# Seven products of halves in place of eight, in three groups of one feed-forward stage

## The chip, the cores and the metric

The kernel runs on one core of one Trainium2 chip. The metric is device time in microseconds of one execution, the median of several runs. A core has TensorE (PE: matmuls; PEld: its weight loads), VectorE (DVE), ScalarE (ACT), GpSimd (POOL) and SyncE (SP), which here issues most DMAs. Each engine works through its own queue in order.

## The reference

Two parts, all in float32 (the feed-forward weights arrive as float64):

```python
# attention: batch 8, heads 12, seq 448, head_dim 64
q_n, k_n = rmsnorm(q, g_q), rmsnorm(k, g_k)
attn = softmax(q_n @ k_n.T / 8)                   # per batch and head
attn_out = attn @ v
x = attn_out.transpose(0, 2, 1, 3).reshape(3584, 768)
# feed-forward: d_model 768, d_ff 1536
g, val = x @ w_gate, x @ w_val
out = (g / (1 + exp(-g)) * val) @ w_out           # (3584, 768)
```

## The kernel before

**Blocks.** The eight batches are taken two at a time, in four blocks `n` = 0 to 3 (the text calls them blocks 1 to 4). A block has an *up* stage (gate and value, `x @ w_gate` and `x @ w_val`), then a *down* stage (`@ w_out`) between whose products the attention of the next block is laid. The last block has no attention beside it.

**Fifteen products.** Both stages use a bilinear scheme for block matrices: a block of 2 batches x 3 thirds of the model width, times a 3 x 3 arrangement of the weights, is formed of 15 products of sums in place of 18. The 15 sums on the side of `x` lie in `xs[:, SLOT[x], c, :]` (128 partitions, `c` = two halves of the contraction of 256, 448 tokens); the sums of the weights are made once, at the beginning, and kept in DRAM (`up_sides`, `down_sides`). `UP_SUMS` and `BLOCKS` give their order there.

**An up stage.** It runs over four groups `g` (128 of the output columns of a third each). In a group, each of the 15 steps of `UP_ORDER` has two products, for the gate and for the value (`which`), and each product is two matmuls (`c` = 0, 1) of a 128 x 128 weight against 448 columns; a float32 matmul is two instructions in the trace. The gate's go to the PSUM banks `mm`, the value's to `at`; within each pair of banks the steps alternate (`b`). After each step its bank is read (L1409 to L1415): by ScalarE where `UP_READ` says `COPY` (6 steps), else by VectorE, which adds it to or takes it from a partial result in SBUF (9 steps), with one further sum per 15 steps (L1528, `add_d`). A bank's next product waits for that read (`free[bank]`). When a gate's result is complete ScalarE forms its SiLU (L1551), and VectorE multiplies it with the value (L1554, `weigh`, into `gt`).

**Weights on the way.** Five steps' weights come in one load into one of two `ws` buffers (L1428), on SP. A load waits in SP's queue for the products that used the buffer before.

**Hand-over.** The down stage's operands are sums of the results (`combine`, L1185 and L1189). `combine(6)` and `combine(1)` are made for each group as soon as its results are there, into `hs`; the first two down products use them.

**The order of the work** is made by `Order`, a planner in the kernel. Each piece of work has an engine, an assumed time, a due time (`when`), what it comes after, and which buffers it takes or uses. The planner lays the pieces out by those assumed times and emits them engine by engine in the order that results. Its times are not seen by the chip: there, only the order in each queue and the waits on data are left. `block_start`, `block_end` and `UP` give the due times; a `rank` moves a piece ahead. `port=True` marks GpSimd work and VectorE work with operands in SBUF, which the planner keeps apart.

## Time and profile before

| | us |
|---|---|
| median of 3 runs | 1454.96 |
| lowest, highest | 1453.89, 1457.8 |
| profiled execution: span from the first to the last instruction | 1452.0 |
| up stage of block 4 in it | 1173.8 to 1354.4 |
| down stage of block 4 and the tail | 1354.4 to 1452.0 |

The page gives no other time of the profiled execution than its span. In the tables that follow, a row of a *group* of instructions has line, engine, operation, tiles (out <- in), shape and count, then the group's busy time, the mean of one in ns, and the idle time of its engine just before them with what ended it. A row of the *timeline* has start, length (both us), engine, line, operation, tiles, shape and count. A row of the *stage table* has the busy time and count of each engine in a stretch, TensorE's granted clock, the DMA share and GB/s. A row of *DMA issues* has size and the median time from issue to landing. A row of *waits* has the total in us, the times and the longest.

### The profile page before, as it was taken

To read this page: it belongs to the slowest core of one execution; us is meant where nothing else is said; L and a number is where in the kernel's file an instruction comes from. 1 tells how busy PE (TensorE), PEld (TensorE's weight loads), DVE (VectorE), ACT (ScalarE), POOL (GpSimd) and SP (SyncE) were. 2 spreads that over 40 slices of the span, in tenths; PEclk is the share of its full clock that TensorE was granted. 3 is DMA by queue.
4 is the path that set the end of the run, shared out by engine and by line. 5 is a ranking of instruction groups with operands and counts; after the bars stand their busy time and mean duration, and the time that the engine had idled before them with its cause. 6 is when DMAs were issued, how large, how long until landed. Compare 5 with 4: busy or idle time off the path is not lost.

```text
span 1452.0 us, 19362 instructions
## 1 busy us (share of the span) xinstructions
PE 1426.0 (98%) x6736; PEld 689.5 (47%) x6736; DVE 879.8 (61%) x1485; ACT 601.6 (41%) x1210; POOL 405.7 (28%) x476
## 2 busy tenths in 40 slices
PE   8999999999999999999999999999999999999997
PEld 4455454534444455544444455544444445555553
DVE  5889876878866434546877642455686644442533
ACT  6875444476653222356564122345555322212100
POOL 4756666625443000022443200011434300000000
PEclk9999999999999999999999999999999999999999
DMA  7778979854643533433644623443463452322235
GB/s 196 217 219 268 352 266 310 260 149 90 129 103 64 133 102 92 114 113 70 122 98 86 138 74 107 107 112 93 85 126 77 95 135 73 108 73 90 69 100 110
DMA packets 410416, 193.29 MB, mean 133 GB/s; under 512 B 280004, under 2 KB 390852, under 8 KB 410308
## 3 DMA queue, kind: packets, MB, share of 16 engines
q1 hardware_dynamic: 399040, 190.57, 49.1%
q10 hardware_dynamic: 11140, 1.38, 0.7%
q8 instruction: 55, 0.90, 0.3%
q14 instruction: 53, 0.43, 0.1%
q0 software_dynamic: 128, 0.00, 0.0%
HBM read 157.29 MB, written 34.60 MB: 132 GB/s over the span
## 4 chain that ended last, share of the span: by engine, by line
PE 90%; DMA 3%; DVE 2%; ACT 2%; SPq 1%; issue 1%; POOL 1%; ACTq 0%; DVEq 0%; POOLq 0%
PE at L1474 25%; PE mm L1474 25%; PE mm L1663 23%; PE at L1049 8%; PE st L970 7%; PE st L1080 1%; PE mm L1080 1%; DMA out_dram<-spare 1%; SPq L768 1%; DMA work<-in_k_dram 1%; ACT es L985 1%; DMA xs<-in_moe_w_gate_dram 0%; PE st L908 0%; DMA v<-in_v_dram 0%; ACT work L918 0%
## 5 line engine op out<-in xcount | busy, mean ns | idle before, releaser
L1474 PE MATMUL at<-xs,ws 128*128 128x448 f32 x960 | 401.2, 540 | 2.5 <-DVE v L1413 1.4
L1474 PE MATMUL mm<-xs,ws 128*128 128x448 f32 x960 | 401.7, 541 | 0.2 <-DVE hs L1315 0.2
L1474 PEld LDWEIGHTS at<-xs,ws 128*128 128x128 f32 x960 | 181.4, 190 | 184.7 <-issue 166.7
L1474 PEld LDWEIGHTS mm<-xs,ws 128*128 128x128 f32 x960 | 182.2, 190 | 180.7 <-issue 177.9
L888 POOL TENSOR_TENSOR work<-work,rr 128x448 f32<-128x448 f32 x72 | 71.8, 1016 | 467.5 <-DVE rr L715 341.6
L1663 PE MATMUL mm<-gt,ws 128*128 128x448 f32 x448 | 175.5, 543 | 0.0
L970 PE MATMUL st<-work 64*64 64x448 f32 (+1 forms) x1536 | 151.2, 501 | 10.3 <-ACT work L918 4.9
L985 ACT ACTIVATE es<-st 128x896 f32<-128x896 f32 x129 | 114.2, 914 | 101.6 <-PE at L1049 87.8
L1411 DVE TENSOR_TENSOR gt<-gt,mm 128x448 f32<-128x448 f32 x64 | 39.7, 621 | 188.1 <-PE mm L1474 161.7
L1663 PE MATMUL mm<-hs,ws 128*128 128x448 f32 x384 | 151.3, 544 | 0.0
L990 POOL TENSOR_TENSOR sums<-es 128x896 f32<-128x896 f32 x36 | 77.2, 2145 | 176.8 <-PE st L1080 83.7
L1663 PEld LDWEIGHTS mm<-gt,ws 128*128 128x128 f32 x448 | 83.6, 190 | 83.0 <-issue 80.8
L1551 ACT ACTIVATE st<-gt 128x448 f32<-128x448 f32 x96 | 52.3, 547 | 159.1 <-DVE gt L1415 85.7
L1409 ACT COPY gt<-mm 128x448 f32<-128x448 f32 x80 | 42.6, 532 | 157.5 <-PE mm L1474 157.4
L1049 PE MATMUL at<-es,v 64*64 64x448 f32 (+1 forms) x1032 | 106.0, 507 | 0.0
L1663 PEld LDWEIGHTS mm<-hs,ws 128*128 128x128 f32 x384 | 71.3, 190 | 71.0 <-issue 70.1
L970 PEld LDWEIGHTS st<-work 64*64 64x64 f32 x1536 | 50.9, 133 | 79.1 <-issue 37.4
L1409 ACT COPY v<-at 128x448 f32<-128x448 f32 x96 | 51.0, 532 | 80.4 <-PE at L1474 79.6
L990 POOL TENSOR_TENSOR sums<-sums,es 128x896 f32<-128x896 f32 x36 | 76.0, 2112 | 2.8
L1049 PEld LDWEIGHTS at<-es,v 64*64 64x64 f32 (+1 forms) x1032 | 44.1, 134 | 56.2 <-issue 50.4
L1554 DVE SCALAR_TENSOR_TENSOR gt<-st,v 128x448 f32<-128x448 f32 x96 | 59.7, 622 | 7.3 <-DVE v L1415 0.5
L1411 DVE TENSOR_TENSOR v<-v,at 128x448 f32<-128x448 f32 x64 | 39.8, 621 | 39.6 <-PE at L1474 39.5
(170 smaller groups left out, 1550.5 us busy)
## 6 DMA issues: line engine op xcount, KB each, us to landing
ws<-up_sides SPq DMA_DIRECT2D x32, 1024.0 KB, 5.6
ws<-down_sides SPq DMA_DIRECT2D x16, 1024.0 KB, 5.7
ws<-down_sides SPq DMA_DIRECT2D x28, 512.0 KB, 4.8
ws<-up_sides SPq DMA_DIRECT2D x16, 768.0 KB, 4.9
out_dram<-spare SPq DMA_DIRECT2D x168, 56.0 KB, 2.1
v<-in_v_dram SPq DMA_DIRECT2D x96, 96.0 KB, 2.5
ws<-up_sides SPq DMA_DIRECT2D x32, 256.0 KB, 5.9
ws<-up_sides SPq DMA_DIRECT2D x16, 512.0 KB, 5.8
```

Of the source, the lines that this page charges most:

```text
L888: nc.gpsimd.tensor_tensor(out=tiles["t", m][:, x], in0=tiles["qk", (m, x)], in1=rr.to_broadcast([P, NC, C]), op=ALU.mult,)
L970: nc.tensor.matmul(st[ds(D * x, D), h, 0:n], tiles["KT", m][rows, ds(P * j + D * of_keys, D)], tiles["QT", m][rows, ds(Q * of_queries, n)] ...
L985: nc.scalar.activation(e, tiles["st", (m, j)][:, :, 0 : S * width(j) // P], AF.Exp)
L990: nc.gpsimd.tensor_tensor(out=to, in0=tiles["e", (m, 0)] if j == 1 else to, in1=e, op=ALU.add)
L1049: nc.tensor.matmul(tiles["at", (m, x)][ds(D * h, D), ds(0, Q) if early else queries], tiles["v", m][rows, j, h], tiles["e", (m, j)][rows, ...
L1080: nc.tensor.matmul(to[ds(D * h + C * x, C)], halves[:, x] if half else many[:, 0:C], term[:, h, 0:Q] if half else term[:, h, ts(x, Q)], st ...
L1409: nc.scalar.copy(to, ps)
L1411: nc.vector.tensor_tensor(out=to, in0=old, in1=ps, op=ALU.add)
L1474: nc.tensor.matmul(ps(), w[:, which, c, at], xs[:, SLOT[x], c], start=fresh and c == 0, stop=c == NC2 - 1, skip_group_check=True,)
L1551: nc.scalar.activation(take(*act, [P, 2, TB])[:, 0, 0:S], to, AF.Silu)
L1554: nc.vector.scalar_tensor_tensor(to, tiles[act][:, 0, 0:S], 1.0 / SCALE, tiles[ready], op0=ALU.mult, op1=ALU.mult,)
L1663: nc.tensor.matmul(banks[s][:, 0:S], w[:, s, g, at], where[x][:, g], start=fresh and g == 0, stop=g == NG - 1, skip_group_check=True,)
```

## The change

**Halves.** In the last block (`SEVEN = {3: (1, 2, 3)}`), groups 1, 2 and 3 treat each of the 15 outer products as a 2 x 2 by 2 x 2 product: tokens in two halves of 224, the contraction in its two halves `c`, and gate and value as the two halves of the columns. That is eight products of 128 x 128 against 224 columns; the new code forms them of seven (Winograd's form), each with operands of its own: A11, A12, A22 of `xs` as they are, and the sums S1 to S4, which GpSimd makes during group 0 (`halves_of`; S3 is written over A21, S1 lies in `hs`, S2 in `work`, S4 in `es`).

**Streams.** The seven are issued as four streams of 15 steps: X and Y and Z two products a step (one bank of 2 x 224 columns), W one. X and Z use the banks `mm`, Y and W the banks `at`. `SEEN` sets when each begins in a group, in thirtieths of it: X 0, Y 6, Z 15, W 21; W of one group runs beside X of the next, and in the last group W's pace is 0.6. `steps`, sorted by due time, is TensorE's order.

**Results.** Each stream is read as before, by `UP_READ`, into partial results of its own. GpSimd adds the streams' results to each other (`combine7`, and `sow` for results 0, 1, 4 and 5); VectorE does `sow` for results 2 and 3. Z's accumulation ends as the gate, W's and Y's as the value.

**Weights.** The differences of the weights that the form needs are made ahead by GpSimd (`prepare`): 8 of 15 pieces during block 2's up stage, 7 during block 3's, each loaded from `up_sides` into `es` or `work`, four GpSimd sums of 384 columns, and a store to `up7`. In the last block the weights are loaded from there into six places (`wp0` to `wp5`, three in each `ws` buffer), three steps at a time for X, Y, Z and six for W. `UP_SUMS` is reordered so that three steps' weights are contiguous. One more buffer (`w6`) is taken from `spare`.

**Hand-over.** `combine(6)` and `combine(1)` of block 4 come after the last Y product (`hs_free`); the banks of its down stage are swapped (`turned_over`). `restore`, which would give A21 back, runs only if a group follows the last of `SEVEN`, so not here.

```diff
-    UP_SUMS = (8, 1, 7, 13, 10, 14, 3, 5, 11, 0, 4)
+    UP_SUMS = (8, 7, 1, 13, 10, 14, 3, 11, 4, 0, 5)
...
+    SEVEN = {3: (1, 2, 3)}
+    HALF = S // 2
...
+    SHORT = 40.0
+    def up_time(n, g=NG):
+        return sum(SHORT if i in SEVEN.get(n, ()) else 30 * PRODUCT for i in range(g))
...
+        def halves_of():
+            for step, x in enumerate(UP_ORDER):
+                before = [old_done[x], *side_done[n, x], down_done.get(n - 1), clusters[EARLY * (n + 1) - 1, "total"]]
+                for i, (to, one, two, op) in enumerate((
+                    ("S3", "A11", "A21", ALU.subtract), ("S2", "A22", "S3", ALU.subtract),
+                    ("S1", "S2", "A11", ALU.add), ("S4", "A12", "S2", ALU.subtract),
+                )):
+                    done = order.add("POOL", 0.55, ..., after=before, port=True, ...)
...
+        PARTS = dict(
+            X=((0, "A11"), (1, "S2")), Y=((1, "S1"), (0, "S3")),
+            Z=((0, "A12"), (1, "A22")), W=((0, "S4"),),
+        )
+        SEEN = dict(X=0.0, Y=6.0, Z=15.0, W=21.0)
...
+            for g in seven:
+                u = (begin[g + 1] - begin[g]) / 30
+                for stream in "XYZW":
+                    pace = 0.6 if stream == "W" and g == seven[-1] else 1.0
+                    for i in range(15):
+                        steps.append((begin[g] + (SEEN[stream] + pace * i) * u, stream, g, i))
+            steps.sort()
...
+            until = [begin[seven[0]] - 30.0] * 3 + [begin[seven[0]]] * 3
+            for (stream, g, u), times in sorted(pieces.items(), key=lambda of: of[1][0]):
+                closing = times[0] > begin[seven[-1]] + 20.0 * (begin[seven[-1] + 1] - begin[seven[-1]]) / 30
+                at = min(range(3 if closing else 0, 6), key=lambda at: until[at])
...
+                done = order.add(
+                    "SP", 0.6, max(times[0] - 12.0, until[at]), load,
+                    after=[*last_load, ...], takes=[key] + ..., early=8.0, rank=SIDES_RANK,
+                )
+                last_load[:] = [done]
+                until[at] = times[-1] + 1.0
...
+                    for side, (_, of) in enumerate(PARTS[stream]):
+                        nc.tensor.matmul(
+                            half(ps(), side), w[side], part_of(of, x),
+                            start=fresh and side == 0, stop=True, skip_group_check=True,
+                        )
+                last = order.add(
+                    "PE", PRODUCT / 4 * n_sides, when, emit,
+                    after=[load, last, free[bank], *(half_done[x, of] for _, of in PARTS[stream] if of[0] == "S")],
+                    uses=[key, tile_of, *held] + ..., mode="full",
+                )
...
+                if stream in "ZW" and result in (0, 4, 5):
+                    before = [sow(result, "POOL", when - 4.0, [last_of(stream, t), seeds[g, stream, result]], seed[result])]
...
+                if stream == "X":
+                    seeds[g, "U2", result] = combine7(("X", t, 1), ("X", t, 1), ("X", t, 0), ...)
+                elif stream == "Y":
+                    u4 = combine7(("Y", t, 0), ("X", t, 1), ("Y", t, 0), ...)
+                    u3 = combine7(("X", t, 1), ("X", t, 1), ("Y", t, 1), ...)
+                    seeds[g, "W2", result] = combine7(("Y", t, 1), ("Y", t, 0), ("Y", t, 1), ...)
+                elif stream == "Z":
+                    if result in (2, 3):
+                        done = sow(result, "DVE", when + 1.0, [done, seeds[g, "Z", result]], ALU.add)
+                    acc["gate", g, result] = done
+                else:
+                    if result in (2, 3):
+                        done = sow(result, "DVE", when + 1.0, [done, seeds[g, "W2", result]], ALU.add)
...
+        def prepare():
+            for j, (g, u) in enumerate(PREPARE[n]):
+                when = start + 4.0 + j * PREPARE_PACE          # 16.0
...
+                done = order.add("SP", 1.0, when, load, ...)
+                for i, (to, one, two) in enumerate(((5, 4, 0), (1, 6, 5), (4, 6, 4), (3, 2, 1))):
+                    done = order.add("POOL", 0.92, when + 8.0 + i, ..., after=[done], port=True, uses=keys[which])
+                up7_done[g, u] = emptied[which] = order.add("SP", 0.6, when + 14.0, ..., after=[done], ...)
...
-            when = start + 30 * (g + 1) * unit + 1.0
-            before = [down_done.get(n - 1)] + ([staged[HS]] if n == 0 else [])
+            when = begin[g + 1] + 1.0
+            before = [hs_free, down_done.get(n - 1)] + ([staged[HS]] if n == 0 else [])
             combine(6, a1, a2, None, when, [hidden[g, 0], hidden[g, 1], *before], g)
             combine(1, b2, h0, ALU.subtract, when, [made[6][g], hidden[g, 4], *before], g)
```

More of the change, by code (lines that the diff above doesn't have):

```diff
@@ L1441, in block @@
         start = block_start(n)
-        unit = (block_end(n) - start) / (30 * NG)
+        unit = PRODUCT + MORE * (n == 0) / (30 * NG)
+        begin = [start + (30 * g * unit if n == 0 else up_time(n, g)) for g in range(NG + 1)]
+        seven = SEVEN.get(n, ())
         last = down_done.get(n - 1)
@@ L1454, in up_product @@
             nonlocal last
-            when = start + (2 * (15 * g + step) + which) * unit
-            b = ("BCDAE".index(CHAIN[x]) % 2 if CHAIN[x] != "E" else 0) ^ (g % 2) ^ (n > 0)
+            when = begin[g] + (2 * step + which) * unit
+            b = ("BCDAE".index(CHAIN[x]) % 2 if CHAIN[x] != "E" else 0) ^ flips[g]
             fresh = x in FRESH
@@ L1571, in up_load @@
             load = add(
-                "SP", 1.2, start + (30 * g + 10 * piece) * unit - 24.0,
+                "SP", 1.2, begin[g] + 10 * piece * unit - 24.0,
                 lambda: load_sides(key, up_sides[g], UP_ORDER[5 * piece :][:5], UP_SUMS),
@@ new lines, in restore @@
+        def restore():
+            for step, x in enumerate(UP_ORDER):
+                side_done.setdefault((n, x), []).append(
+                    order.add(
+                        "POOL", 0.55, third_done[x]["when"] + 1.0,
+                        lambda x=x: nc.gpsimd.tensor_tensor(
+                            out=part_of("A21", x), in0=part_of("A11", x), in1=part_of("S3", x),
+                            op=ALU.subtract,
+                        ),
+                        after=[third_done[x]], port=True,
+                    )
+                )
@@ L1588, in block @@
                 up_product(g, step, UP_ORDER[step], which, load, key)
+                old_done[UP_ORDER[step]] = last
+            if seven and g == seven[0] - 1:
+                halves_of()
+        if n in PREPARE:
+            prepare()
         up_done[n] = last
@@ L1687, in emit_read @@
                     old = tiles[value]
-                read(how, tiles[value], old, banks[s][:, 0:S])
+                read(how, tiles[value], old, banks[s ^ turned_over][:, 0:S])
             done = add(
```

283 lines of the change are left out of this document (275 added, 8 removed).

## The prediction

> **What bounds the kernel now.** I read the page's head and its chain of waits first, then a table of busy times by stage, then the groups of instructions of the last block's up stage, then single rows of the timeline around the places that the change touches.
>
> ```profile
> span 1452.0 us, 19362 instructions
> ...
> PE 1426.0 (98%) x6736; PEld 689.5 (47%) x6736; DVE 879.8 (61%) x1485; ACT 601.6 (41%) x1210; POOL 405.7 (28%) x476
> ...
> PE 90%; DMA 3%; DVE 2%; ACT 2%; SPq 1%; issue 1%; POOL 1%; ACTq 0%; DVEq 0%; POOLq 0%
> ```
>
> TensorE sets the end: 98% busy, 90% of the chain. So a change is worth what it takes from TensorE, less what it puts in as waits of TensorE. The stage table has the up stages of blocks 2 and 3, groups 1, 2 and 3 of the last up stage, and the last down stage with the tail.
>
> ```profile
> core 0: us, PE busy (x) PEld busy (x) DVE busy (x) ACT busy (x) POOL busy (x), PEclk, DMA share, GB/s
> 479.60:665.10 185.50, 185.50 (x530) 92.57 (x529) 81.61 (x144) 64.24 (x123) 11.94 (x10) 1.00 0.38 102
> 826.90:1012.40 185.50, 185.50 (x530) 92.55 (x529) 81.66 (x144) 64.20 (x123) 11.94 (x10) 1.00 0.39 102
> ...
> 1218.90:1264.10 45.20, 45.20 (x122) 22.88 (x121) 17.18 (x28) 9.67 (x18) 0.00 (x0) 1.00 0.27 88
> 1264.10:1309.20 45.10, 45.10 (x122) 22.80 (x121) 17.18 (x28) 9.67 (x18) 0.00 (x0) 1.00 0.27 88
> 1309.20:1354.40 45.20, 45.20 (x122) 22.90 (x121) 17.18 (x28) 9.67 (x18) 0.00 (x0) 1.00 0.27 82
> 1354.40:1452.00 97.60, 90.19 (x240) 45.23 (x239) 39.23 (x43) 6.39 (x12) 0.00 (x0) 0.97 0.43 99
> ```
>
> A group holds 120 matmul instructions in 45.15 us with no hole: 0.376 us each at a granted clock of 1.00. VectorE works 17.2 of the 45 us, GpSimd not at all. The hand-over to the down stage has no hole either; and a bank is read 0.20 us after its product's slot ends (product 1229.44 to 1230.95, read at 1231.15):
>
> ```profile
> 1229.44 1.67 PE L1474 MATMUL at<-xs,ws 128*128 128x448 f32 x4
> 1230.95 1.67 PE L1474 MATMUL mm<-xs,ws 128*128 128x448 f32 x4
> ...
> 1231.15 0.53 ACT L1409 COPY v<-at 128x448 f32<-128x448 f32 x1 [0.97 <-PE at L1474]
> ...
> 1352.72 1.67 PE L1474 MATMUL at<-xs,ws 128*128 128x448 f32 x4
> 1354.22 2.04 PE L1663 MATMUL mm<-hs,ws 128*128 128x448 f32 x5
> ```
>
> **Term 1, the products.** For each of 15 outer products in 3 groups, 8 instructions of 448 columns (gate and value, two K halves, two passes) become 14 of 224 columns (seven products, two passes). No row has 224 columns against a 128 x 128 weight. The nearest have narrower weights; the others time the weight load alone.
>
> ```profile
> L1049 PE MATMUL at<-es,v 128*64 128x224 f32 x168 | 18.2, 357 | 0.0
> ...
> 44.83 2.06 PE L1049 MATMUL at<-es,v 128*64 128x224 f32 x20
> ...
> 8.42 0.19 PEld L1756 LDWEIGHTS mm<-rr,ident 112*128 112x128 f32 x1 [0.19 <-issue]
> 8.53 0.30 PEld L1756 LDWEIGHTS mm<-work,ident 112*128 112x128 f32 x2
> ```
>
> The 20 run as ten pairs, one on each half of the array's columns: (2.06 - 0.357)/9 = 0.189 us from pair to pair, half of 0.376 and 1 ns. Two 128-column loads start 0.11 us apart (8.42, 8.53; and two in 0.30 that last 0.19 each). So a load needs 0.11 us of a 0.189 us matmul that covers it. Bounds: 0.189 if it is hidden, 0.189 + 0.11 = 0.30 if none is. I take 0.189, since in the pairs two loads are hidden under one such matmul. A group: 15 x 14 x 0.189 = 39.7 us in place of 45.1; three groups: **-16.2 us**; if none is hidden, 630 x 0.11 = 69 us the other way.
>
> The Trainium skill speaks against this: "TensorE: Matmul & The Clock Gate", section "Back-to-back issue gap", has about 81 ns per matmul at 128 columns in a stream of load and matmul pairs, where a matmul alone takes 56. An estimate from that page, 25 ns on each of 630 instructions, would be 15.8 us, all of the gain. No run here shows it; the pairs above show none of it.
>
> **Term 2, the group's beginning.** X (two products of 224, one bank of 448) runs alone for its first six steps; Y joins at 6 units of 1.33 us. A step is 4 x 0.189 = 0.756 us, and its bank is wanted again one step later, but the read ends 0.20 + 0.53 (ScalarE) or 0.20 + 0.62 (VectorE) after it. That is 0.73 to 0.82 against 0.756, with a hop of a few hundredths and a weight load (0.11) that starts late: **+0.8** for six steps (0 to 2). It happens in group 1 only; later X runs beside W.
>
> **Term 3, VectorE's queue.** The durations of what it does:
>
> ```profile
> L1554 DVE SCALAR_TENSOR_TENSOR gt<-st,v 128x448 f32<-128x448 f32 x18 | 11.2, 624 | 1.6
> L1411 DVE TENSOR_TENSOR gt<-gt,mm 128x448 f32<-128x448 f32 x12 | 7.5, 622 | 51.6 <-PE mm L1474 51.4
> L1528 DVE TENSOR_TENSOR gt<-gt,w 128x448 f32<-128x448 f32 x3 | 1.9, 626 | 0.1
> ...
> L1303 DVE TENSOR_SCALAR st<-es 128x576 uint32<-128x576 uint32 x8 | 6.0, 755 | 0.1
> L1303 DVE TENSOR_SCALAR mm<-hs 128x384 uint32<-128x384 uint32 x6 | 3.4, 558 | 0.1
> ...
> L1528 DVE TENSOR_TENSOR gt<-gt,w 128x448 f32<-128x448 f32 x16 | 12.1, 756 | 0.5
> ```
>
> From 558 at 384 columns and 755 at 576, a read of 224 takes 0.39. A group has 27 full and 9 half reads, 3 full and 1 half add of `d`, 2 full and 2 half sums of Z and W with the earlier parts (`sow`), 6 weighings: 16.8 + 3.5 + 2.3 + 2.0 + 3.7 = 28.3 us of 39.7. Eight of them take both inputs from SBUF while GpSimd now works, and such a one waits for the GpSimd instruction in flight:
>
> ```profile
> 780.48 0.92 DVE L1189 TENSOR_TENSOR xs<-xs 128x448 f32<-128x448 f32 x1
> ...
> 779.07 1.84 POOL L888 TENSOR_TENSOR work<-work,rr 128x448 f32<-128x448 f32 x2 [4.57 <-DVE rr L715]
> ...
> L1336 POOL TENSOR_TENSOR es<-es 128x128 f32<-128x128 f32 x20 | 8.6, 455 | 0.3
> L888 POOL TENSOR_TENSOR work<-work,rr 128x448 f32<-128x448 f32 x72 | 71.8, 1016 | 467.5 <-DVE rr L715 341.6
> ```
>
> The vector sum of 0.62 lasted 0.92 and ended with GpSimd's second (779.07 + 1.84 = 780.91; it may overlap its end a little). I take 0.3 us for each of the eight, 2.4 a group; bounds 0 and the whole of a 224-column GpSimd sum, 0.6 (between 455 ns at 128 and 1016 at 448 columns). GpSimd has 24 sums of 0.6, 4 of 1.0 and 4 of 0.6 a group: 21 of 39.7 us, so it keeps up. Together VectorE is at 77%, but unevenly. Z steps 10 to 14 run beside W steps 4 to 8 for 5 x (0.756 + 0.378) = 5.7 us, and bring 5 reads, an add and a sum of 0.62, 4 half reads, a half sum and a weighing: 6.9 us, and 0.9 of waits. A Z bank has 1.5 us until it is wanted and needs 1.0, so of 2.1 us too much 0.5 is absorbed: 1.5. In the next stretch (W 9 to 14 beside X 0 to 5, 6.8 us) the same count gives 7.7 us, mostly weighings, for which nothing on TensorE waits: 0.25. Groups 1 and 2: **+3.5** (0 to 12: none if the reads always go first, twice the excess in both stretches if weighings and late GpSimd sums go ahead of them).
>
> **Term 4, the last group's loads.** The six places `wp0` to `wp5` take the weights of three steps each (384 KB). In the middle a place is free 8.3 us before its next weights are used. For pieces that begin after 20 units of the last group, `range(3 if closing else 0, 6)` leaves three places. By the code's own times Z's third piece then gets its place 0.3 us ahead, W's second 1.1, W's third (192 KB) 1.9.
>
> ```profile
> ws<-up_sides SPq DMA_DIRECT2D x32, 1024.0 KB, 5.6
> ...
> work<-in_q_dram SPq DMA_DIRECT2D x144, 56.0 KB, 2.3
> work<-in_q_dram SPq DMA_DIRECT2D x12, 224.0 KB, 3.9
> ```
>
> For 384 KB a line from 56 to 1024 KB gives 3.4 us, one from 224 to 1024 gives 4.2; I take 3.8, and 3.3 for 192 KB. Between the last use of the place and the first of the new weights TensorE has one Z and one W step (1.1 us, less a hop: 1.0), one Z and two W (1.4), and two Z and three W (2.6, less a hop: 2.5): waits of 2.8, 2.4 and 0.8. **+6.0** (1.8 if they land in 2.3; 11.9 if in 5.6).
>
> The Trainium skill, "DMA: Bandwidth & Descriptors", section "Anatomy of one DMA — SWDGE (gpsimd) path", fits 2.0 us plus bytes at 436 GB/s for a neighbouring kind of queue: 2.9 us for 384 KB as an estimate, and the term would be 3.5. The 1024 KB row takes 1.2 us more than that fit.
>
> **Term 5, the hand-over.** `combine(6)` and `combine(1)` of groups 0 to 2 now wait for the last Y product, since S1 lies in `hs`. From there to the down stage VectorE has, of Z, 7 reads, an add and 2 sums (6.2 us), of W half of each of these and 2 reads more (9 x 0.39 + 3 x 0.39 = 4.7), six waits of 0.3, three weighings and seven combines that the first down product needs (10 x 0.62), and a read in hand: 19.5 us. TensorE has 9 Z and 15 W steps and the waits of term 4: 12.5 + 6.0 = 18.5. So VectorE is late by 1.0, and the down product, behind a hop and a weight load, by a little more: **+1.5** (0 to 7, the latter if the loads are not late and VectorE alone is). The product of 6 then lasts 6 us, under which the rest is caught up.
>
> **Edits costed at nothing.** Block 4's halves: 60 GpSimd sums of 0.6, 36 us within group 0's 45; X's first step needs the first of them 40 us later. Weight differences in blocks 2 and 3: 60 sums of 0.85 in two stages of 185.5 us, where GpSimd has 11.9; 15 loads (of one or two transfers) and 15 stores on SP. In an up stage SP waits for TensorE anyway, as in the last block's:
>
> ```profile
> SPq L1428 <- PE at L1474: 158.4, 12, 13.7
> ```
>
> A piece of weights lasts TensorE 15 us and lands 5.6 after its place is free, so a store that waits on SP for GpSimd has 9.4 us of cover; beyond it, each microsecond is one of TensorE. **+0.3** (0 to 4). `UP_SUMS` in another order and the swapped banks of the last down stage change no count.
>
> **The sum.** -16.2 + 0.8 + 3.5 + 6.0 + 1.5 + 0.3 = -4.1 on the profiled span of 1452.0: 1447.9. The page gives no other time for that execution; the median of the runs, 1454.96, lies 2.96 above the span, and I keep that: **1450.9 us**. What this kernel's measurement can tell from no change is 0.3%, 4.4 us; the forecast lies at its edge.
>
> **The rivals.**
> A. *The late loads and the full queue are absorbed.* Landing in 3 us leaves 2.0 + 1.6 + 0.2 in term 4; terms 2, 3 and 5 are 0.5 each: -16.2 + 3.8 + 1.5 = -10.9, 1444. For it: VectorE's 77%. Against: three rows of landing, all but the smallest above 3.
> B. *VectorE becomes the bound of all three groups.* The planner chains each load after the landing of the one before, 54 in all, and so fills VectorE's order as though TensorE paused between them; a weighing then stands ahead of a read. With 4.5 us in each of three groups: -16.2 + 0.8 + 13.5 + 6.0 + 1.5 + 0.3 = +5.9, 1460.9. It turns slower from 2.5 us a group on, and by more than 0.3% from 4.0. Against: the rows above put reads every 0.756 us, of which VectorE has three in five.
> C. *A weight load shows under the short matmul* (slower). If a fifth of the 0.11 us shows, 630 x 0.022 = 14 us: +10, 1465. It decides from 4.1/630 = 6.5 ns on, a spacing of 0.1955. Against it, the pairs and the two loads above. The rule that term 1 cites from the Trainium skill is this one.
> D. *SP's queue in blocks 2 and 3.* A store that holds it over 9.4 us, four times by 2 us: +8 - 4.1, 1459. Against: the cover.
> That the change does not do what it says: if 448-column instructions stayed, so would the time; the code leaves no such way, and I give it no chance.
>
> **How the numbers follow.** Forecast (-9 to +1) 0.56, A 0.16, B 0.14, C 0.07, D 0.07. Faster by over 0.3%: 0.29 of the forecast's and all of A, 0.45. Within: 0.27 and part of B and D, 0.36. Slower: C, most of B, part of D, 0.19. Range 1443.5 to 1462: from A's time to B's; the forecast's own is 1446 to 1456.
>
> **What would show it.** 630 up matmuls of 224 columns beside 1560 of 448, 0.189 us apart where they run undisturbed; TensorE's idle in groups 1 and 2 released by VectorE, about 2 us each; in the last 12 us of the up stage, TensorE released by `ws<-up7`, about 6 us in all; the first down product released by VectorE; up stages of blocks 2 and 3 still 185.5. The prediction is wrong if the short matmuls are over 0.195 apart, if TensorE does not wait for `ws` at the end, or if VectorE holds it for over 12 us in groups 1 and 2.

## The result and the profile after

| | ratio to before, 95% interval | median, us | span of the profiled execution, us |
|---|---|---|---|
| before | 1 | 1455.13 | 1452.0 |
| after | 1.0126 [1.0109, 1.0144] | 1474.88 | 1472.2 |

The median of before is here that of four runs, one more than the three whose median the forecast starts from. The change makes the kernel 20 us slower by the medians; the forecast was 4 us faster, and the range ended at 1462.0. The head of the page and its chain of waits, kernel after:

```profile
span 1472.2 us, 20483 instructions
...
PE 1426.7 (97%) x7006; PEld 734.6 (50%) x7006; DVE 918.6 (62%) x1557; ACT 616.3 (42%) x1246; POOL 576.1 (39%) x692
...
PE 83%; DVE 4%; DMA 3%; POOL 3%; ACT 2%; SPq 2%; issue 1%; POOLq 0%; ACTq 0%; DVEq 0%
```

TensorE's share of the chain fell from 90% to 83%; VectorE and GpSimd took most of it. The stage table answers where. Its rows are the up stage of block 2, groups 1, 2 and 3 of the last up stage, the last down stage with the tail, and two short stretches inside group 3. A group is here 210 instructions of TensorE in a row.

```profile
core 0: us, PE busy (x) PEld busy (x) DVE busy (x) ACT busy (x) POOL busy (x), PEclk, DMA share, GB/s
482.45:667.72 185.27, 185.23 (x528) 92.13 (x527) 81.78 (x144) 63.68 (x122) 43.76 (x42) 1.00 0.64 195
...
1221.90:1269.80 47.90, 44.30 (x211) 37.52 (x210) 23.60 (x41) 12.96 (x27) 25.30 (x36) 1.00 0.49 152
1269.80:1317.10 47.30, 44.48 (x212) 37.58 (x212) 27.51 (x50) 14.46 (x30) 23.10 (x32) 1.00 0.47 146
1317.10:1371.30 54.20, 46.54 (x211) 38.25 (x211) 33.31 (x60) 13.96 (x29) 24.55 (x32) 0.97 0.39 119
1371.30:1472.20 100.90, 90.80 (x242) 45.49 (x240) 43.80 (x52) 8.54 (x16) 0.00 (x0) 0.98 0.42 96
...
1361.00:1362.00 1.00, 1.00 (x6) 0.91 (x5) 0.44 (x1) 0.08 (x1) 1.00 (x2) 0.72 0.00 0
1362.00:1364.00 2.00, 2.00 (x7) 1.57 (x5) 1.14 (x4) 0.00 (x0) 0.80 (x2) 0.50 0.00 0
```

A group of 210 short instructions would last 39.7 us at 0.189 us each. The three last 149.4 in place of 119.1: 30.3 us of holes and slow stretches eat the 16.2 saved and leave 14 us lost against before's 135.5 (14.4 from the first up product to the last, 194.43 against 180.02). A hole is, in this text, the time from the end of an instruction's 0.189 us to the start of the next; the wait that the profile gives for it is up to 0.2 us shorter. The down stage and tail are 2.8 us longer than the 98.2 they took before (from the last up product's start). The other 3 us of the span lie ahead of the last up stage, which starts at 1176.84 in place of 1173.82; 2.1 of them are in block 1's up stage. Block 2's up stage, with GpSimd now busy for 43.8 us in it, lasts 185.27 from its first product to its last in place of 184.96, and block 3's 184.96 as before.

What the holes look like is seen in the timeline of group 1, where X's and Y's steps alternate:

```profile
1237.14 0.65 PE L1737 MATMUL at<-hs,ws 128*128 128x224 f32 x2
...
1237.62 0.54 PE L1737 MATMUL at<-xs,ws 128*128 128x224 f32 x2
...
1238.20 0.62 DVE L1427 TENSOR_TENSOR spare<-spare,at 128x448 f32<-128x448 f32 x1
1238.38 0.54 PE L1737 MATMUL mm<-work,ws 128*128 128x224 f32 x2
1238.87 0.30 PEld L1737 LDWEIGHTS at<-hs,ws 128*128 128x128 f32 x2 [0.30 <-DVE spare L1427]
1238.88 0.65 PE L1737 MATMUL at<-hs,ws 128*128 128x224 f32 x2
```

A pair of steps should last 8 x 0.189 = 1.51 us; this one lasts 1.74. The product at 1238.88 writes one of the two `at` banks, and it starts 0.06 us after VectorE's read of the *other* one ends (1238.20 + 0.62). Its weight load starts only then as well, and two short matmuls that follow a wait take 0.65 in place of 0.54. In the code the two banks are one tensor, `at_banks = psum.tile([P, 2, TB], ...)`, while the two `mm` banks are two.

Why this cost nothing in the last up stage of before can be read from the rows of before: the read of `at` that starts at 1231.15 lasts 0.53, and a gate product of 1.504 us lies between two value products. In the new kernel the cover is an X step of 0.756 us, and 0.20 + 0.62 + 0.06 is 0.88.

Three of the larger waits of TensorE in the last block (total, times, longest), for the hand-over's sums and for weights:

```profile
PE mm L2046 <- DVE hs L1200: 2.8, 1, 2.8
PE mm L1737 <- DVE hs L1204: 2.4, 1, 2.4
...
PE at L1737 <- DMA ws<-up: 2.0, 1, 2.0
```

### The profile page after: what moved, and what is told of

The parts are those of the page before. It is cut to its first block, busy times and chain, and to the rows that moved or that the text cites. A ratio compares the mean times of both kernels' runs of the same rounds, so it can differ in the third digit from the quotient of the medians.

```text
span 1472.2 us, 20483 instructions
## 1 busy us (share of the span) xinstructions
PE 1426.7 (97%) x7006; PEld 734.6 (50%) x7006; DVE 918.6 (62%) x1557; ACT 616.3 (42%) x1246; POOL 576.1 (39%) x692
## 4 chain that ended last, share of the span: by engine, by line
PE 83%; DVE 4%; DMA 3%; POOL 3%; ACT 2%; SPq 2%; issue 1%; POOLq 0%; ACTq 0%; DVEq 0%
PE mm L2046 22%; PE at L1492 19%; PE mm L1492 19%; PE at L1064 7%; PE st L985 7%; PE at L1737 3%; PE mm L1737 3%; SPq L783 2%; PE st L1095 1%; PE mm L1095 1%; DMA work<-in_k_dram 1%; DMA out_dram<-spare 1%; ACT es L1000 1%; DMA ws<-up_sides 1%; POOL spare L1868 1%
## 5 line engine op out<-in xcount | busy, mean ns | idle before, releaser
L1492 PE MATMUL at<-xs,ws 128*128 128x448 f32 x780 | 326.2, 541 | 4.7 <-DVE v L1429 3.6
L1492 PE MATMUL mm<-xs,ws 128*128 128x448 f32 x780 | 327.1, 542 | 0.4 <-DMA ws<-up_sides 0.2
L1492 PEld LDWEIGHTS at<-xs,ws 128*128 128x128 f32 x780 | 147.2, 190 | 153.4 <-issue 135.0
L1492 PEld LDWEIGHTS mm<-xs,ws 128*128 128x128 f32 x780 | 148.1, 191 | 147.9 <-issue 144.5
L1427 DVE TENSOR_TENSOR gt<-gt,mm 128x448 f32<-128x448 f32 x64 | 39.7, 620 | 141.3 <-PE mm L1492 110.4
L1569 ACT ACTIVATE st<-gt 128x448 f32<-128x448 f32 x78 | 42.4, 546 | 119.9 <-DVE gt L1431 65.2
L1939 POOL TENSOR_TENSOR es<-es 128x384 f32<-128x384 f32 x32 | 31.2, 997 | 103.2 <-DMA es<-up_sides 102.5
L1737 PE MATMUL mm<-xs,ws 128*128 128x224 f32 x270 | 67.4, 359 | 3.8 <-DVE hs L1204 2.4
L1425 ACT COPY v<-at 128x448 f32<-128x448 f32 x78 | 41.5, 532 | 62.9 <-PE at L1492 62.1
```

Source lines behind the costliest of these rows:

```text
L1425: nc.scalar.copy(to, ps)
L1427: nc.vector.tensor_tensor(out=to, in0=old, in1=ps, op=ALU.add)
L1492: nc.tensor.matmul(ps(), w[:, which, c, at], xs[:, SLOT[x], c], start=fresh and c == 0, stop=c == NC2 - 1, skip_group_check=True,)
L1569: nc.scalar.activation(take(*act, [P, 2, TB])[:, 0, 0:S], to, AF.Silu)
L1737: nc.tensor.matmul(half(ps(), side), w[side], part_of(of, x), start=fresh and side == 0, stop=True, skip_group_check=True,)
L1939: lambda raw=raw, to=to, one=one, two=two: nc.gpsimd.tensor_tensor(out=raw[:, to], in0=raw[:, one], in1=raw[:, two], op=ALU.subtract),
```

## The experiments

Theories at the start. **A**: the two `at` banks are one tensor, so every Y or W step waits for the read of the step before. **VectorE**: it simply has too much to read (the prediction's rival B). Later came **G** (GpSimd's sums stand in the wrong order), **L** (the closing weights land late, term 4) and **H** (VectorE's order at the hand-over, term 5). The runs were made in four sets, each with its own runs of the kernel before (medians 1454.4 to 1455.5), to which the ratios refer.

**1. Two tensors.** Where another part of the kernel reads both banks in one operation, it now takes two.

```diff
-    at_banks = psum.tile([P, 2, TB], F32, name="at", bufs=1)
+    at_banks = [psum.tile([P, TB], F32, name=f"at{i}", bufs=1) for i in range(2)]
...
-            tiles[name, key] = at_banks[:, at]
+            tiles[name, key] = at_banks[at][:, :]
...
-                nc.vector.tensor_tensor(out=to, in0=to, in1=at_banks[:, :, 0:Q], op=ALU.mult)
+                for i in range(2):
+                    to = x[:, ts(i, Q)]
+                    nc.vector.tensor_tensor(out=to, in0=to, in1=at_banks[i][:, 0:Q], op=ALU.mult)
```

> The changed kernel with the value's two PSUM banks as two tensors (at0, at1) in place of one tensor of two banks; the early attention's last multiplication, which read both banks at once, becomes two of half the width. Theory A (one tensor): in the changed kernel each Y and W step waits for the read of the step before it, in the other bank, because both banks are one tensor; TensorE lost 23.8 us of its 30.4 us of holes ahead of these steps. Without that, groups 1 and 2 go from 47.9 and 47.3 us to 41 to 42.5 each, group 3 from 54.2 to about 50, the last up stage from 194.4 to about 176; the run is at 1454 to 1459. Theory B (VectorE's queue is what is late): the waits move to the true bank and stay; groups 1 and 2 at 46 or more, the run at 1470 to 1476.

Measured: 1.0024 [1.0013, 1.0035], 1458.15 us. TensorE in the stretch that answers to the one above:

```profile
1235.13 0.54 PE L1738 MATMUL at<-xs,ws 128*128 128x224 f32 x2
...
1235.89 0.54 PE L1738 MATMUL mm<-work,ws 128*128 128x224 f32 x2
1236.27 0.54 PE L1738 MATMUL at<-hs,ws 128*128 128x224 f32 x2
1236.64 0.54 PE L1738 MATMUL at<-xs,ws 128*128 128x224 f32 x2
```

Two instructions every 0.38 us, 0.189 each, without a hole: theory A holds for X beside Y. By the starts of the products, less 0.189 us each, 23.8 of the 30.4 us lost in the three groups stood ahead of Y's and W's products; here it is 6.8 of 21.4, and none of it ahead of Y's. Yet groups 1 and 2 last 47.35 and 45.45 us where some 42 were expected, 0.5 and 1.8 less than with the one tensor, and only group 3 gained much (47.48 in place of 54.2). The total lies in its range in part by luck: in the trace the last block starts 4.3 us sooner than in the changed kernel's, which was not expected. What is left in groups 1 and 2 is mostly one hole each, and what follows it. Stage table and timeline:

```profile
1217.62:1264.97 47.35, 43.98 (x212) 41.54 (x210) 23.88 (x40) 12.96 (x27) 25.22 (x36) 0.93 0.49 155
1264.97:1310.42 45.45, 42.34 (x211) 40.70 (x211) 27.88 (x50) 14.46 (x30) 23.14 (x32) 0.96 0.48 148
...
1257.80:1259.00 1.20, 1.20 (x3) 1.13 (x4) 0.75 (x2) 0.00 (x0) 0.50 (x1) 0.50 0.00 0
1259.00:1264.00 5.00, 5.00 (x15) 4.53 (x15) 2.38 (x5) 0.35 (x1) 0.66 (x1) 0.53 0.21 49
1264.00:1266.00 2.00, 2.00 (x12) 2.00 (x12) 1.41 (x4) 1.13 (x3) 0.00 (x0) 1.00 0.19 75
```

```profile
1255.94 1.13 POOL L1805 TENSOR_TENSOR gt<-gt,v 128x448 f32<-128x448 f32 x1
...
1257.10 1.16 DVE L1432 TENSOR_TENSOR gt<-mm,gt 128x448 f32<-128x448 f32 x2 [2.43 <-POOL gt L1805]
1257.78 1.86 PE L1738 MATMUL mm<-xs,ws 128*128 128x224 f32 x4 [2.41 <-DVE gt L1432]
```

The chain is read backwards: X's product waits for a bank, the bank for VectorE's read of Z's result 0, that read for GpSimd's sum (`sow`, L1805) that ends at 1257.07. GpSimd had come to it late, through fifteen sums of `combine7` in a row. Behind the hole the granted clock is 0.50 to 0.53 for 6 us, and some 16 instructions take 0.18 us more each: 2.9 us. This profiled execution took 1461.05 us, 2.9 above the run's median; whether the others lose as much here is not shown.

**2. The kernel before with two tensors**, to know what the split is worth without the change.

> The kernel before with the same two tensors. Theory A: the value's product waits for the read of the other bank there too, but the gate's product of 1.50 us covers the 0.9 us; so the same time within 2 us (1453 to 1457), the last up stage still 180.0 us. Theory B says the same here; a gain of over 3 us would say that the kernel before paid for it too, in its first block or in attention.

Measured: 0.9973 [0.9961, 0.9984], 1450.61 us; the expectation missed. The last up stage is unchanged (180.02 us), but block 1's up stage takes 192.34 us in place of 193.84 and the last block starts 3.3 us sooner: the single tensor had cost the old kernel something too, outside the change.

**3. VectorE's work cut.** The sums and weighings on VectorE with operands in SBUF, 18 a group, made 32 columns wide in place of 448 or 224; the rest of their columns is left out.

```diff
+                        if engine == "DVE":
+                            to, one, two = to[:, 0:32], one[:, 0:32], two[:, 0:32]
...
-                            gt[:, g, result], tiles[act][:, 0, 0:S], 1.0 / SCALE, tiles[ky],
+                            gt[:, g, result][:, 0:32], tiles[act][:, 0, 0:32], 1.0 / SCALE, tiles[ky][:, 0:32],
```

> The changed kernel (one tensor), where in groups 1 to 3 of the last block VectorE's sums of Z and W with the earlier parts, its adds of d and its weighings work on the first 32 columns alone: 18 of its instructions a group take some 0.1 us, 8 us less a group. It leaves out most of these sums and of the products of gate and value, and its output is not the reference's. Theory A: groups 1 and 2 stay at 45.5 to 47, since X/Y pairs have little of this work and wait all the same. Theory B: they fall to 40 to 42.

Measured in a single run: 1464.62 us; groups of 46.75, 45.32 and 52.22 us. VectorE's amount is not the bound of the groups: with much of its work gone they keep 5.6 to 12.5 us of holes. It is not free either: the last up stage is 5.0 us shorter than the changed kernel's. Of the other 4.5 us between the two traces 3.1 lie ahead of the last block, where the edit touches nothing.

**4. The new order of the weights, with no seven products.**

```diff
-    SEVEN = {3: (1, 2, 3)}
+    SEVEN = {}
```

Nor are the differences made (`PREPARE` is empty).

> The changed kernel with no group of seven products and no weight differences: what is left of the change is the new order of the weights' sums in DRAM, the new due times' code and the two added buffers. The changed kernel is 3.0 us late when its last block begins, nearly all of it from the first block. If that comes from the order of the weights' sums or the other order of queues in the first block: about 1458 (1456.5 to 1460). If it comes from the GpSimd work of blocks 2 and 3, or from chance of that one execution: 1453.5 to 1456.5.

Measured: 0.9996 [0.9985, 1.0008]. `UP_SUMS` and the rest of the planner's new order cost nothing that can be measured. In its one trace block 1's up stage takes 195.73 us, as in the changed kernel (195.93); that the runs' time is level all the same says that the 3 us that the changed kernel loses ahead of its last block in one trace can't be put to an edit.

**5. Two tensors, and the third combination later** (theory G), in groups 1 and 2: only W needs these sums, which stood ahead of the sums that Z's first read waits for.

```diff
-                    seeds[g, "W2", result] = combine7(("Y", t, 1), ("Y", t, 0), ("Y", t, 1), when + 2.4, [u3], [ky])
+                    if g == seven[-1]:
+                        seeds[g, "W2", result] = combine7(("Y", t, 1), ("Y", t, 0), ("Y", t, 1), when + 2.4, [u3], [ky])
...
                     acc["gate", g, result] = done
+                    if g != seven[-1]:
+                        seeds[g, "W2", result] = combine7(
+                            ("Y", t, 1), ("Y", t, 0), ("Y", t, 1), when + 2.4, [seeds[g, "Z", result], done], [ky],
+                        )
```

> The changed kernel with the two result banks of the halves as two tensors, and with the last seven-product sums of groups 1 and 2 (the third combination, that only the product of the second correction bank needs) recorded after the sums that empty the bank of the first product. Theory G (the holes of 2.6 us in groups 1 and 2 of the run with two tensors come from sums on GpSimd that stand ahead of the emptying ones, and the 2.9 us of slower matmuls behind each from the clock that falls in the hole): both holes gone, granted clock 1.00 through groups 1 and 2, group 1 at 41 to 43 us and group 2 at 40 to 41.5, group 3 as before at 46 to 48; the run at 1445 to 1450. Rival (GpSimd as a whole is too slow, some 25 us of sums and their waits in a group): the hole moves to the second correction product and stays at 2 us or more; groups 1 and 2 at 44 to 47, the run at 1454 to 1459.

```profile
1218.89:1260.99 42.10, 41.26 (x212) 39.00 (x211) 24.05 (x41) 12.95 (x27) 24.55 (x36) 1.00 0.55 173
1260.99:1302.46 41.47, 40.88 (x211) 39.24 (x210) 27.94 (x51) 14.50 (x30) 23.25 (x33) 1.00 0.54 167
1302.46:1349.95 47.49, 42.78 (x210) 40.24 (x210) 33.24 (x60) 14.20 (x29) 25.39 (x33) 0.96 0.43 135
```

Measured: 0.999 [0.998, 0.9999], 1452.78 us. Groups 1 and 2 meet the forecast, at a granted clock of 1.00, with GpSimd busy for much the same time as in run 1 (24.55 and 23.25 us after 25.22 and 23.14): theory G, and the order, not the amount. The total is 2.8 us above its range; group 3 is unchanged at 47.49.

**6. The third combination later, with the one tensor.**

> The changed kernel with its one tensor of two banks, and only the third combination of groups 1 and 2 recorded later. If the one tensor alone makes the 12.5 and 11.3 us of short waits (theory A), those stay, and what goes is 1 to 4 us in each of groups 1 and 2: the run at 1467 to 1473. If GpSimd's order were the main cause of the loss, groups 1 and 2 would come to 41 to 43 us and the run to 1461 to 1464.

Measured: 1.014 [1.0122, 1.0158], 1474.55 us; groups of 47.29, 46.98 and 54.04 us. The expectation missed, for less went than either theory had set: with the one tensor GpSimd's order costs 0.3 to 0.6 us a group. The losses don't add. Group 1 lasts 47.87 us in the changed kernel, 47.35 with two tensors, 47.29 with the later combination and 42.10 with both, so either cause alone holds it near 47, and only the two repairs together free it. TensorE's waits for the read that needs GpSimd's sum, first of the changed kernel, then of run 1, fit this: under the slower steps GpSimd is hardly late.

```profile
PE mm L1737 <- DVE gt L1431: 0.4, 2, 0.2
...
PE mm L1738 <- DVE gt L1432: 4.8, 2, 2.4
```

**7 and 8. The closing loads given places further ahead** (theory L), with two tensors and the later combination, and with the one tensor.

```diff
-                closing = times[0] > begin[seven[-1]] + 20.0 * (begin[seven[-1] + 1] - begin[seven[-1]]) / 30
+                closing = times[0] > begin[seven[-1]] + 22.0 * (begin[seven[-1] + 1] - begin[seven[-1]]) / 30
```

> As the run both, and the loads of the closing group get places further ahead (the threshold at which a step takes a load 22 in place of 20). Theory L (the two holes of 2.2 us in group 3 are pieces of the weights that land late because their places lie 0.3 and 1.1 us ahead of their use): both holes gone, the clock stays at 1.00, group 3 at 40.5 to 43.5 us and 4 to 6 us less in all than the run both: 1439 to 1445. Rival (the loads are late because of the buffers' readers or of the other transfers, not of the places): holes of over 1.5 us stay ahead of the same products, within 1.5 us of the run both.

> The changed kernel with its one tensor of two banks, and only the threshold of the closing loads at 22 in place of 20. Theory L: the hole of 2.19 us ahead of the second piece of the second correction bank and the half clock behind it go, groups 1 and 2 stay at 47 to 48 us: the run 2 to 4 us below the changed kernel's, 1470 to 1473. Rival (the loads' places matter little): within 1.5 us of the changed kernel, the hole stays.

Measured: both_closing 0.9976 [0.9964, 0.9988], 1452.06 us; closing 1.0116 [1.0094, 1.0138], 1472.55 us. TensorE's waits, first of both, then of both_closing:

```profile
PE mm L1738 <- DMA ws<-up: 2.2, 1, 2.2
PE at L1738 <- DMA ws<-up: 1.8, 1, 1.8
```

```profile
PE at L1738 <- DVE spare L1430: 2.4, 1, 2.4
```

The waits for `ws<-up` are gone, as theory L has it, and with the one tensor too (group 3 of closing 51.44 us in place of 54.2). But the run with two tensors gains 0.7 us and not 4 to 6: at the place of the first of the two waits there is now one for VectorE, which the load had hidden. VectorE's rows ahead of it:

```profile
1331.35 0.85 DVE L1201 SCALAR_TENSOR_TENSOR hs<-gt 128x448 f32<-128x448 f32 x1
...
1332.24 0.96 DVE L1205 TENSOR_TENSOR hs<-gt,hs 128x448 f32<-128x448 f32 x1
...
1333.13 1.07 DVE L1201 SCALAR_TENSOR_TENSOR hs<-gt 128x448 f32<-128x448 f32 x1
...
1334.23 0.97 DVE L1205 TENSOR_TENSOR hs<-gt,hs 128x448 f32<-128x448 f32 x1
...
1335.13 0.61 DVE L1430 TENSOR_TENSOR spare<-spare,at 128x448 f32<-128x448 f32 x1
```

Four sums of the hand-over for groups 0 and 1, 0.85 to 1.07 us each beside GpSimd, stand ahead of a read that TensorE waits for. They have long been due by the planner's clock, since `hs` only comes free in group 3; a read's rank of 60 us doesn't overcome that.

**9 and 10. Those sums due at the end of the up stage** (theory H), and then the weighings of results 0 and 1 first.

```diff
+            late = [begin[NG] - 5.0, begin[NG] + 1.0] if n == NB - 1 else [when, when]
-            combine(6, a1, a2, None, when, [...], g)
-            combine(1, b2, h0, ALU.subtract, when, [...], g)
+            combine(6, a1, a2, None, max(when, late[0]), [...], g)
+            combine(1, b2, h0, ALU.subtract, max(when, late[1]), [...], g)
...
                         "DVE", 0.62, when + 1.0, weigh, after=[gated, done, seeds[g, "W2", result]], uses=[act, ky],
+                        rank=60.0 * (g == seven[-1] and result < 2),          # run 10 only
```

> As the run both_closing, and in the last block the sums that the first two down products need of groups 0 to 2 are due at the end of the up stage (5 us before it, and 1 us after it) in place of right behind each group, so that reads, which the planner puts first by 60 us, go ahead of them. Theory H (the hole of 2.60 us in group 3 is VectorE's four sums of groups 0 and 1 in a row ahead of a read, 0.85 to 1.07 us each, and the ten matmuls 0.18 us slower behind it are the clock): that hole and the slower ones gone, group 3 at 41 to 43 us in place of 46.0. At the hand-over the six weighings in a row (3.6 us) stay ahead of the sums and the sums come later: the hole there is 2 to 5 us in place of 1.8. The run 1 to 4 us below both_closing: 1448 to 1451. Rival (VectorE has too much to do in group 3 whatever its order): the hole moves within group 3, which stays at 45 to 47 us: 1451 to 1454.

> As sums_late, and the weighings of results 0 and 1 of group 3, that the first down product waits for, go first by the same 60 us as the reads. Theory H: the hole at the hand-over comes to 0 to 1.5 us, group 3 stays at 41 to 43: 1446.5 to 1449.5. Rival (the hand-over is bound by the number of VectorE's instructions and not by their order): 2 us or more stay there, within 1 us of sums_late.

Measured: 0.9977 [0.9964, 0.9991] and 0.9968 [0.9956, 0.998], 1451.04 and 1450.63 us; group 3 takes 45.06 and 45.43 us, the wait for the hand-over's sums is 3.1 and 2.7. Both missed. The wait of 2.4 us went, and the clock stays at 1.00, but holes of 1.5 and 1.8 us came up in the same group, and at the hand-over four weighings still stood ahead of the sums: the rival's reading, "the hole moves within group 3", is the better one for these two.

**11 and 12. What the repaired kernel is to be measured by**: the old kernel with two tensors once more, and the same with the weight differences made in blocks 2 and 3 and not used.

> The kernel before with the two result banks as two tensors, once more, as the measure for the seven products with all repairs: 4 to 5 us below the kernel before, as the first time (0.9973). If seven products with the repairs are worth something beside eight with the same two tensors, sums_late_weigh is below this one by 1 us or more; if what they cost outside the products (the differences made in blocks 2 and 3, the hand-over) takes all of it, they are level or above.

> Two tensors, the weight differences made in blocks 2 and 3 and stored, and the last block with eight products of whole tiles, which leaves the differences unused: what the differences cost by themselves. Forecast from single traces: one load of the up weights in block 2's up stage lands late by 0.2 to 1.8 us and nothing else changes: 0.5 to 2 us above before_two_banks_again. If they cost nothing, within 0.5 us of it; if they hold SP's queue again and again (rival D of the prediction), 4 us or more above it.

Measured: 0.9979 [0.997, 0.9989], 1451.65 us, and 0.9993 [0.9981, 1.0005], 1453.06 us. The differences cost 1.4 us by the medians, as forecast, with intervals that overlap. Run 10, of the same set, is 1.0 us below the old kernel with two tensors, again with intervals that overlap: by that alone seven products are not shown to pay. The trace of run 12 has one wait for late weights in the up stage of block 2:

```profile
PE mm L1493 <- DMA ws<-up_sides: 0.8, 1, 0.8
```

In other traces of the series that wait is 0.2 to 2.1 us. So one load is late, and SP's queue is not held four times (rival D). That the load lands late beside `prepare`'s own transfers is a reading that no run separates; the median landing of the 1024 KB loads is 5.8 us in this trace, 5.6 before.

**13 and 14. The hand-over in the order of need**, and the third combination later in group 3 too.

```diff
-            late = [begin[NG] - 5.0, begin[NG] + 1.0] if n == NB - 1 else [when, when]
+            late = [begin[NG] - 20.0, begin[NG] + 5.0] if n == NB - 1 else [when, when]
...
-                        rank=60.0 * (g == seven[-1] and result < 2),
+                        rank=(g == seven[-1]) * (60.0 if result < 2 else -3.0),
```

> As sums_late_weigh, with the rest of VectorE's work at the hand-over in the order in which the down products need it: the sums of the first down product due from 20 us before the end of the up stage, those of the second 5 us after it, and the four weighings that the first doesn't need 3 us later. Theory H: the hole ahead of the first down product comes from 2.8 us to 0.5 to 1.5, group 3 stays at 45 to 45.5 us: 1448.5 to 1450. Rival (VectorE's number of instructions there is the bound): 2.5 us or more stay.

> As last_orders, and the third combination is recorded behind the emptying sums in group 3 too. Theory G for group 3 (its hole of 1.82 us, released by VectorE's read of the second Z bank that waits for GpSimd's sum of result 0, is GpSimd's order as in groups 1 and 2): that hole gone, group 3 at 42 to 44 us, the run 1 to 3 us below last_orders. Rival (in group 3 the last products of the second correction wait for the third combination, which now comes late): as long a hole ahead of those, group 3 unchanged or longer, the run level with last_orders or above.

Measured: last_orders 0.9957 [0.9942, 0.9972], 1448.47 us, all but as expected; last_orders_later 0.9952 [0.9939, 0.9965], 1448.68 us. Stage table of last_orders, groups 1 to 3, and TensorE's wait at the hand-over:

```profile
1216.47:1258.58 42.11, 41.26 (x212) 39.00 (x210) 24.06 (x41) 12.94 (x27) 24.55 (x36) 1.00 0.55 173
1258.58:1300.06 41.48, 40.89 (x212) 39.24 (x212) 27.96 (x51) 14.50 (x30) 23.26 (x33) 1.00 0.54 167
1300.06:1344.75 44.69, 41.15 (x211) 39.06 (x210) 33.22 (x59) 14.58 (x30) 25.86 (x33) 1.00 0.46 144
```

```profile
PE mm L1738 <- DVE gt L1432: 1.0, 1, 1.0
PE mm L2054 <- DVE hs L1201: 1.0, 1, 1.0
```

At the hand-over it was the order: the same instructions, and the wait for `hs L1201` is 1.0 us where it was 2.7. Run 14 takes the wait for `gt L1432` away, as theory G has it, but a row of three hand-over sums (3.51 us) slips ahead of a read and makes a hole of 1.80 with a half clock behind it; group 3 lasts 45.23 us, and the time is level: the rival's outcome, by another mechanism than the rival named.

This is a version that beats both kernels: some 6 us below before. Against the old kernel with two tensors (0.9973 and 0.9979) it is 2 to 3 us below by the medians, with intervals that overlap at their ends and from different sets of runs; that seven products pay beside eight is likely by this and not shown.

## Why the prediction was wrong

**Term 1 (-16.2)** was right. Where nothing disturbs, the short instructions stand 0.189 us apart (two in 0.38 above), so the rival C fell: groups of 42.1 and 41.5 us (runs 5 and 13) are the 39.7 and some short waits. By the prediction's estimate from the Trainium skill ("TensorE: Matmul & The Clock Gate", section "Back-to-back issue gap"), 25 ns on each instruction, a group would be 5 us longer than 39.7; these rows do not show it.

**Term 3 (+3.5, 0 to 12)** is the step that failed. Groups 1 and 2 lost 8.2 and 7.6 us in place of 1.75 each; the first holds term 2's 1.6 as well. The term counted what VectorE has to do in a stretch against the stretch, and gave each bank the time until it is wanted itself, which holds for `mm` and not for `at`: as one tensor the two banks are waited for together, so the time was one step of 0.756 us and not three. Run 1 shows it: the holes ahead of Y's products, 11.3 us in all, are gone with two tensors. The same rows of before that the prediction quotes hold both halves of the sum, a read that ends 0.73 after the product's end and 1.504 us of cover; the new cover was never set against them for Y beside X, as term 2 does for X alone. The line `psum.tile([P, 2, TB], ...)` was there to be read. Nor did GpSimd "keep up". Its amount was forecast roughly (21 us, and it is busy for 25.3), but a sum that a bank waits for stood behind fifteen others, five of which only W needs. Run 5 shows that, once the one tensor no longer hides it. One reading of the term's rows is off too: the vector sum that starts at 780.48 ends at 781.40, 0.49 us after GpSimd's second, and not with it; the 0.3 us of stretch stands.

**Rival B** had the size in its direction (a VectorE-bound group from 4 us on) but not the cause: run 3 takes VectorE's work away and the groups stay at 45 to 47 us. Its sentence that a planned order can set a sum ahead of a read came true in group 3 alone.

**Term 4 (+6.0)** had its mechanism. The places were too few by the code's own times, and W's second piece made TensorE wait 2.02 us where 2.4 was forecast (a hole of 2.19). Z's third was forecast at 2.8; the wait at its place, 2.4 us, ends with VectorE's sums in this trace, and the load's own holes in the runs with two tensors are 2.2 and 2.4. W's third (0.8) was not waited for. The lower bound of 1.8 was summed wrongly: by the prediction's own covers of 1.0, 1.4 and 2.5, a landing of 2.3 leaves 2.2. Landing was sized at 3.8; the row after has

```profile
ws<-up SPq DMA_DIRECT2D x51, 384.0 KB, 3.3
```

against 2.9 by the estimate from the Trainium skill ("DMA: Bandwidth & Descriptors", section "Anatomy of one DMA — SWDGE (gpsimd) path") that the prediction gave: the measured row lies between the two. Left out was the clock: after the hole for W's second piece the rows 1361:1364 above run at 0.72 and 0.50, by which they lose 0.28 x 1 + 0.50 x 2 = 1.3 us.

**Term 5 (+1.5)** measured 2.8, the wait for `hs L1200`: six weighings in a row (3.62 us) ahead of the last sums. It counted only the three weighings that the first down product needs; the order put all six ahead. Run 13 shows that the order makes most of it.

**Term 2 (+0.8) and the edits at nothing (+0.3)** held: X alone at the start of group 1 loses 1.6 us in this trace and 1.2 with two tensors, inside 0 to 2; and in block 2 there is one late load of 0.2 us in this trace, up to 2.1 in others, inside the range of 0 to 4.

The sum by stages: 3.0 us ahead of the last block, which run 4 doesn't tie to any edit, 14.4 in the last up stage and 2.8 behind it make the 20.2 us between the spans. The 14.4 are -16.2 and 30.3 of holes and slow stretches, and some tenths of rounding and of group 0. The 30.3 stand in place of the 10.3 that terms 2, 3 and 4 had, the 2.8 in place of 1.5.

## What to carry to other kernels

When work is cut into shorter pieces, set every read that a piece waits for against the new cover, one by one, and look up how the buffers are declared: two banks in one tensor are waited for as one. Then look for the sum that somebody waits for now behind those that are wanted later; the share of busy time of the engine says nothing of it. And expect repairs to uncover each other: run 7 took 4.0 us of waits away and gained 0.7.

## What the runs showed of the hardware

**The clock can fall behind holes of some 2 us.** Behind several waits of 2.0 to 2.4 us the granted clock was 0.50 for 3 to 6 us, and a short instruction took 0.37 us in place of 0.189 (1257.80:1264.00 above). The Trainium skill, "TensorE: Matmul & The Clock Gate", section "HAM oscillation — how this bites in real kernels", has a rule of no idle gap over about 3.4 us; here waits of 2.41 us, and in run 14 one of 1.64, sufficed. Not every one did it: after the second wait for `ws<-up` in run 5 (1.8 us), after VectorE's 2.39 us in group 3 of the changed kernel and after 2.22 us in group 3 of run 8 the next matmuls were at full pace. Rows of the changed kernel from 1350 on, its wait of 2.39 us among them, then of run 14:

```profile
1350.00:1355.00 5.00, 2.52 (x12) 2.04 (x12) 4.93 (x8) 1.22 (x4) 4.60 (x6) 1.00 0.39 146
...
1346.00:1349.00 3.00, 3.00 (x10) 2.71 (x9) 2.12 (x6) 0.21 (x1) 3.00 (x6) 0.50 0.80 226
```

So the length of a single hole doesn't decide it; what else does, no run here separates.

**A wait costs 0.10 us beyond itself.** The weight load starts only when the wait ends (0.30 in place of hidden, row 1238.87), so the two matmuls behind take 0.65 in place of 0.54. Where each of the 45 Y steps waits, that alone is 4.5 us, worked out from these rows.

**VectorE's sums in SBUF stretch by 0.2 to 0.45 us beside GpSimd.** The prediction took 0.3 us for each; four in a row took 0.85, 0.96, 1.07 and 0.97 in place of 0.62, and the starts lie 0.9 to 1.1 us apart.
